# A gated FFT convolution, forward and backward: ScalarE's 4 KB transfers on SyncE's queue, gradients stored by channel halves, taps loaded into 32 rows, a new order

## The chip, the cores and the metric

The kernel runs on one core of one Trainium2 chip. A core has a matrix engine (TensorE, PE in the profile; its weight loads are PEld), VectorE (DVE), ScalarE (ACT), GpSimd (POOL) and SyncE (SP), and 16 DMA engines that move data between memory and the core's buffer. Each engine works off its own list of instructions in program order. SyncE and ScalarE issue transfers, each on a queue of its own (q1 and q10 in the page). The metric is the device time of one execution in microseconds.

## The reference

The sequence has 2048 positions and D = 512 channels; the feed-forward part has F = 1376 columns. `q`, `k`, `v` and `grad_out` are bfloat16 arrays of 2048 x 512.

```python
def _A_ref(q, k, v, shift_k, ssm_k, ssm_D):
    for t in range(4):                      # four taps per channel, along the sequence
        k_shift = k_shift + k_pad[:, t:t + S, :] * shift_k[:, 3 - t]
    kv = k_shift * v
    kv_f = rfft(kv padded to 4096); kf_f = rfft(ssm_k padded to 4096)
    y = irfft(kv_f * kf_f)[:2048]           # a long convolution, per channel
    return q * (y + kv * ssm_D)

def _B_ref(x, w_gate, w_up, w_down):
    return (sigmoid(x @ w_gate) * (x @ w_up)) @ w_down

xn = _layernorm(q)
out = q + _A_ref(xn, k, v, shift_k, ssm_k, ssm_D) * silu(_B_ref(xn, w_gate, w_up, w_down))
```

The kernel returns `out` and the gradients of `q`, `k`, `v`, the taps `shift_k`, the long filter `ssm_k`, `ssm_D` and the three weight matrices: `out_0`, then `out_1` to `out_9` in this order.

## The kernel before

**Layout.** Position 16p + j lies in partition p, slot j (`cview`, NJ = 16). The channels are worked in four groups of 128 (`NG`, `GW`). A Fourier transform of length 4096 is done as matmuls with constant tables: `step1`, a transpose by VectorE in 32 x 32 blocks (`flip`) and `step2` one way, `inv2` and `inv1` back. The spectra of the long filter (KD) and of the value path (VD) are written to memory on the way forward and loaded again on the way back, in two halves for each group.

**Stages.** First come the input loads, the layer norm of the first rows, and constant tables made by GpSimd and VectorE out of index patterns (`gen_fft_tables`, `gen_fft_consts`), while TensorE multiplies zeros (`warm`) until the first real matmul. Then the gate and up projections and the forward convolution, interleaved; then the backward pass of the feed-forward part. The last stage, from about 290 us on, has three parts that run interleaved:

- `dW` computes the weight gradients. Its operand tiles come by transposing loads from memory (`hD`, `dgD`, `duD`; the last twelve are `duD`) into three buffers. Its results go through five output buffers (`ot_r`), and ScalarE issues their stores (`out_7` to `out_9`, 128 KB each).
- `frontC` takes the gradient of the convolution's output through the forward transform, group by group.
- `backC` does the rest of the backward convolution, group by group: it loads the filter rows `ksh` (512 KB, one piece of 4 KB for each partition), multiplies the spectra, transforms back, writes the value gradient in place in `y2A`, stores the filter gradient `out_5` (512 KB, again 4 KB pieces), and computes the key gradient `dk` in `zA`. `ksh` and `out_5` are issued by ScalarE. The value gradient `out_3` is stored at the last group, whole; the key gradient `out_2` at the last group in two halves of the slots.

**The taps.** Four loads put the 4 x 512 taps of each group into one row each (rows 0, 32, 64, 96) of a tile `skr` that GpSimd has cleared (a memset of 128 x 2048). A matmul with 32 rows of ones (`ones1`) spreads them over all partitions (`skbc`).

**What sets the order.** A recorder (`Rec`) collects the operations of all stages with their numbers. Then `order` lays them out by tables of numbers: `ORDER` has one list for each engine, in which `a+n` stands for a, a+1, ..., a+n, and a list "moves" that fixes the order of the transfers over all queues. An evacuation of an accumulator (`evac`) goes to ScalarE or VectorE, by the list in which its number stands. A second table, `BANKS`, gives each accumulator its place. All instructions are issued in `emit`, so that every row of the profile has its line, L506.

Of the kernel before, what the change touches and what calls it, by code (L numbers as in the profile page):

```python
# [26 lines left out]
NG = 4  # L27
GW = D // NG
# [47 lines left out]
    """,  # L76
    "vector": """
# [555 lines left out]
def kernel_impl(ctx, tc, A_q, A_k, A_v, A_shift_k, A_ssm_k, A_ssm_D, B_x, B_w_gate, B_w_up, B_w_down,  # L633
                grad_out, out_0, out_1, out_2, out_3, out_4, out_5, out_6, out_7, out_8, out_9):
    nc = tc.nc
# [730 lines left out]
    def backC():  # L1366
        for cg in range(NG):
# [32 lines left out]
            if cg == NG - 1:  # L1400
                nc.sync.dma_start(o3C, y2A)
# [127 lines left out]
```

## Time and profile before

| what | value |
|---|---|
| median of three runs | 455.55 us (455.09, 455.55, 455.56) |
| the profiled execution | 456.14 us |
| its span, from the first to the last instruction | 454.3 us |
| mean granted TensorE clock | 0.996 of full speed |
| TensorE busy | 439.6 us (97% of the span) |
| VectorE busy | 410.4 us (90%) |
| ScalarE busy | 287.7 us (63%) |
| GpSimd busy | 23.2 us (5%) |
| data moved by DMA | 117.13 MB, mean 258 GB/s |
| share of the 16 DMA engines' span, SyncE's queue and ScalarE's | 89.3% and 6.6% |

Times are microseconds from the start of the span. A row of the timeline gives the start, the length, the engine, the operation with its tiles (result <- source), and in brackets the idle time of the engine before it and what ended that. `slab` is the one buffer in which all tiles lie; names such as `KD`, `duD` and `kshD` are arrays in memory, and `out_dram` any output. A wait is put down to what came last. A row with `x2` and more joins neighbours of one form. The share of the DMA engines can stand a little above 1 in a window.

### The profile page before, as it was taken

The numbers are of one execution on the slowest core, as the hardware profiler recorded it, in microseconds if no ns is written. First come the engines' busy times: TensorE is split into PE (matmuls) and PEld (weight loads), VectorE is DVE, ScalarE is ACT, GpSimd is POOL, SyncE is SP. The second block draws the span as 40 slices with busy tenths as digits, with TensorE's granted clock in tenths as the row PEclk, the third lists the DMA queues.
The fourth block names the chain that finished last, engine by engine and source line by source line (L and its number), as shares of the span: only waits on it lengthen the run. The fifth ranks groups of instructions, "written<-read, shape, count | busy, mean of one in ns | idle before, by whom it ended". The sixth has DMA issues, their size and how long they took to land.

```text
span 454.3 us, 11795 instructions
## 1 busy us (share of the span) xinstructions
PE 439.6 (97%) x4996; PEld 305.8 (67%) x5031; DVE 410.4 (90%) x620; ACT 287.7 (63%) x357; POOL 23.2 (5%) x49
## 2 busy tenths in 40 slices
PE   7999999999999999999999999999999999699997
PEld 3786686777768668566665755445577888588796
DVE  7899998999989999999999897779899999599992
ACT  4788788979787446973654433447567756475432
POOL 6501020000000000000000000000000000000000
PEclk9899999999999999999999999999999999999999
DMA  7988999649659889999998999899999999999996
GB/s 268 301 281 224 283 342 301 200 164 279 215 193 302 242 227 210 300 299 326 295 313 240 304 257 255 251 269 226 264 233 211 287 226 221 266 183 286 194 335 239
DMA packets 188678, 117.13 MB, mean 258 GB/s; under 512 B 107418, under 2 KB 174930, under 8 KB 188114
## 3 DMA queue, kind: packets, MB, share of 16 engines
q1 hardware_dynamic: 178320, 107.56, 89.3%
q10 hardware_dynamic: 10306, 8.82, 6.6%
q8 instruction: 39, 0.64, 0.6%
q14 instruction: 13, 0.11, 0.1%
HBM read 43.74 MB, written 46.70 MB: 199 GB/s over the span
## 4 chain that ended last, share of the span: by engine, by line
PE 88%; DMA 4%; DVE 2%; ACT 2%; issue 1%; POOL 1%; SPq 0%; ACTq 0%; POOLq 0%; DVEq 0%
PE psum L506 88%; DVE slab L506 2%; DMA slab<-duD 2%; DMA slab<-KD 2%; ACT slab L506 2%; POOL slab L506 1%; SPq L506 0%; ACTq L506 0%; POOLq L506 0%; DVEq L506 0%; POOLq L1513 0%
## 5 line engine op out<-in xcount | busy, mean ns | idle before, releaser
L506 PE MATMUL psum<-slab 128*128 128x256 bf16 (+5 forms) x4996 | 439.6, 302 | 11.3 <-DVE slab L506 6.0
L506 PEld LDWEIGHTS <-slab 128*128 128x128 bf16 (+2 forms) x5031 | 305.8, 96 | 145.0 <-issue 38.4
L506 ACT CAST slab<-psum 128x1024 bf16<-128x1024 f32 (+3 forms) x227 | 197.3, 907 | 130.3 <-PE psum L506 103.9
L506 DVE TENSOR_TENSOR slab<-slab 128x1024 bf16<-128x1024 bf16 (+4 forms) x302 | 240.5, 832 | 14.3 <-ACT slab L506 6.2
L506 ACT ACTIVATE slab<-slab 128x512 bf16<-128x512 bf16 (+5 forms) x63 | 53.3, 875 | 23.1 <-DVE slab L506 22.5
L506 DVE STREAM_TRANSPOSE slab<-slab 128x1024 f32<-128x1024 f32 x48 | 64.7, 1354 | 2.6 <-PE psum L506 1.7
L506 DVE CAST slab<-psum 128x1024 bf16<-128x1024 f32 (+2 forms) x38 | 42.4, 1119 | 11.5 <-PE psum L506 11.2
L506 DVE TENSOR_TENSOR slab<-psum,slab 128x512 bf16<-128x512 f32 (+2 forms) x52 | 31.7, 612 | 6.7 <-ACT slab L506 5.4
L506 ACT ACTIVATE slab<-psum 128x512 bf16<-128x512 f32 (+1 forms) x48 | 27.4, 576 | 6.6 <-PE psum L506 6.4
L506 POOL MEMSET slab<- 128x128 bf16 (+4 forms) x11 | 6.0, 559 | 255.5 <-DVE slab L506 152.1
L506 POOL TENSOR_TENSOR slab<-slab 128x2 f32<-128x2 f32 (+3 forms) x11 | 11.0, 1006 | 100.2 <-DVE slab L506 100.1
L506 DVE SCALAR_TENSOR_TENSOR slab<-slab 128x2 f32<-128x2 f32 (+2 forms) x41 | 14.5, 363 | 0.3
L506 ACT ACT_TABLE_LOAD x10 | 12.8, 1283 | 1.9 <-PEq L1513 1.7
L506 DVE SCALAR_TENSOR_TENSOR slab<-psum,slab 128x512 bf16<-128x512 f32 x16 | 10.8, 686 | 1.2 <-ACT slab L506 1.1
L506 DVE TENSOR_SCALAR slab<-slab 128x512 bf16<-128x512 bf16 (+6 forms) x26 | 8.4, 335 | 2.9 <-POOL slab L506 2.8
L506 DVE BATCH_NORM_STATS2 slab<-slab 128x6 f32<-128x512 bf16 x16 | 10.7, 676 | 0.0
L506 ACT COPY slab<-psum 128x1024 bf16<-128x1024 bf16 (+2 forms) x9 | 7.5, 837 | 1.5 <-PE psum L506 1.5
L506 DVE COPY slab<-psum 128x512 bf16<-128x512 bf16 (+1 forms) x10 | 4.8, 494 | 0.1
L506 POOL TENSOR_SCALAR slab<-slab 128x1 f32<-128x1 f32 (+3 forms) x10 | 3.3, 337 | 0.4
L506 DVE BATCH_NORM_AGGREGATE slab<-slab 128x2 f32<-128x6 f32 x16 | 2.7, 172 | 0.1
L506 DVE MEMSET slab<- 32x192 uint32 (+3 forms) x10 | 1.6, 160 | 1.2 <-PEq L1513 0.9
L506 POOL IOTA slab<- 128x32 f32 (+3 forms) x8 | 2.1, 272 | 0.5 <-POOLq L1513 0.4
(12 smaller groups left out, 7.1 us busy)
## 6 DMA issues: line engine op xcount, KB each, us to landing
slab<-KD SPq DMA_DIRECT2D x16, 512.0 KB, 4.6
hD<-slab SPq DMA_DIRECT2D x8, 704.0 KB, 6.2
dgD<-slab SPq DMA_DIRECT2D x8, 704.0 KB, 5.3
duD<-slab SPq DMA_DIRECT2D x8, 704.0 KB, 5.2
slab<-in_A_k_dram SPq DMA_DIRECT2D x4, 1024.0 KB, 7.0
KD<-slab SPq DMA_DIRECT2D x8, 512.0 KB, 4.7
VD<-slab SPq DMA_DIRECT2D x8, 512.0 KB, 4.4
out_dram<-slab SPq DMA_DIRECT2D x16, 256.0 KB, 3.9
```

What stands on the lines that cost most here:

```text
L506: getattr(getattr(self.nc, eng), meth)(*[place(v) for v in a], **{x: place(v) for x, v in k.items()})
```

## The change

Six places in the code are edited, and the tables are replaced.

1. GpSimd's memset of `skr` is gone. Each tap load fills 32 rows with the same 4 x 128 taps (a source stride of 0), and `ones1` holds 1/32 in place of 1.
2. The loads of `ksh` go from ScalarE's queue to SyncE's.
3. So do the stores of `out_5`.
4. `out_3` leaves in two stores of 256 channels each, recorded at the second and at the fourth group, where it was one store.
5. `out_2` leaves in one store of 256 channels, recorded at the second group, and at the fourth in two stores of eight slots and 256 channels each; before, in two stores of eight slots and 512 channels.
6. All lists in `ORDER`, and `BANKS`, are new. The lists name 588 operations for VectorE before and 589 now, 394 and 385 for ScalarE, 5031 and 5031 for TensorE, 237 and 247 for SyncE, 45 and 44 for GpSimd. Some 50 evacuations change their engine.

```diff
 ORDER = {
     "tensor": """
-        28 19 26 25 22 17 20 24 7+7 21 160+7 170+7 16 15 23 44+3 27 49+3 198+7 187+7 257+7 122+15 236+15 179+7 207+7
+        18 25 16 24 7+7 159+7 26 169+7 28 27 49+3 44+3 15 17 19 22 235+15 23 293+7 21 256+7 321+7 301+7 312+7 265+7
...
@@ -863,15 +864,15 @@
     f_ld(1)
     ld_w(256, 768, nc.sync, nc.sync)
-    nc.gpsimd.memset(skr, 0.0)
     for r in range(4):
-        nc.sync.dma_start(skr[32 * r:32 * r + 1, r, :], A_shift_k[r * GW:(r + 1) * GW, :].rearrange("(o d) t -> o (d t)", o=1))
+        taps = A_shift_k[r * GW:(r + 1) * GW, :]
+        nc.sync.dma_start(skr[32 * r:32 * r + 32, r, :], bass.AP(taps.tensor, taps.offset, [[0, 32], [1, 4 * GW]]))
     ld_w(768, F, nc.sync, nc.sync)
...
-    nc.gpsimd.memset(ones1, 1.0)
+    nc.gpsimd.memset(ones1, 1.0 / 32)
@@ -1370,7 +1371,7 @@
             ksh = ksh_r.next()
-            nc.scalar.dma_start(ksh.rearrange("p j d -> p (j d)"), kshD[cg])
+            nc.sync.dma_start(ksh.rearrange("p j d -> p (j d)"), kshD[cg])
@@ -1397,8 +1398,8 @@
             nc.vector.tensor_tensor(dkv, dkv, ksh, ALU.mult)
-            if cg == NG - 1:
-                nc.sync.dma_start(o3C, y2A)
+            if cg % 2 == 1:
+                nc.sync.dma_start(o3C[:, :, c1 - 2 * GW:c1], y2A[:, :, c1 - 2 * GW:c1])
@@ -1409,7 +1410,7 @@
-            nc.scalar.dma_start(out_5[c0:c1, :], dKT.rearrange("p n j -> p (n j)"))
+            nc.sync.dma_start(out_5[c0:c1, :], dKT.rearrange("p n j -> p (n j)"))
@@ -1436,8 +1437,8 @@
-                if cg == NG - 1:
-                    nc.sync.dma_start(o2C[:, js, :], zA[:, js, :])
+                if cg % 2 == 1:
+                    nc.sync.dma_start(o2C[:, js, c1 - 2 * GW:c1], zA[:, js, c1 - 2 * GW:c1])
```

The tables' effect is seen in the order of the instructions. First SyncE's queue in the last stage, from the load of the value rows (`in_A_v`) of groups 2 and 3 on; `duD` are the transposing loads for `dW`, KD3 and VD3 the spectra of group 3, `in_A_k` the key rows, `slab<-slab` a shift of three rows between partitions. Before:

```order
L506 DMA slab_102<-in_A_v_dram 128x16x256
L506 DMA_TRANSPOSE slab_102<-duD0_97 128x8x256
L506 DMA slab_102<-slab_102 15x384
L506 DMA_TRANSPOSE slab_102<-duD1_98 128x8x256
L506 DMA slab_102<-KD3_64 128x2048 x2
L506 DMA slab_102<-in_A_k_dram 112x3x256
L506 DMA_TRANSPOSE slab_102<-duD0_97 128x8x256 x2
L506 DMA_TRANSPOSE slab_102<-duD1_98 128x8x256 x2
L506 DMA slab_102<-VD3_68 128x2048
L506 DMA slab_102<-in_A_k_dram 15x3x256
```

The same stretch now, up to the second half of the key spectrum (`kshD2` is the `ksh` load of group 2):

```order
L507 DMA slab_102<-in_A_v_dram 128x16x256
L507 DMA slab_102<-KD3_64 128x2048
L507 DMA_TRANSPOSE slab_102<-duD0_97 128x8x256
...
L507 DMA slab_102<-kshD2_59 128x2048
...
L507 DMA_TRANSPOSE slab_102<-duD1_98 128x8x256
L507 DMA out_5_dram<-slab_102 128x2048
L507 DMA_TRANSPOSE slab_102<-duD0_97 128x8x256
L507 DMA_TRANSPOSE slab_102<-duD1_98 128x8x256
L507 DMA_TRANSPOSE slab_102<-duD0_97 128x8x256
L507 DMA_TRANSPOSE slab_102<-duD1_98 128x8x256
L507 DMA_TRANSPOSE slab_102<-duD0_97 128x8x256
...
L507 DMA slab_102<-KD3_64 128x2048
```

The first load of KD3 has moved ahead of two transposing loads, the second one behind seven; `ksh` and an `out_5` store stand among them (a row shift and two key halos between these rows are left out).

Second, the end of the same queue, before:

```order
L506 DMA_TRANSPOSE slab_102<-duD0_97 128x8x128
L506 DMA slab_102<-slab_102 112x384
L506 DMA out_3_dram<-slab_102 128x8192
L506 DMA slab_102<-slab_102 15x384
L506 DMA_TRANSPOSE slab_102<-duD1_98 128x8x128
L506 DMA out_2_dram<-slab_102 128x4096 x2
```

and now:

```order
L507 DMA_TRANSPOSE slab_102<-duD1_98 128x8x256 x2
L507 DMA out_3_dram<-slab_102 2048x1x256
L507 DMA out_5_dram<-slab_102 128x2048
L507 DMA slab_102<-slab_102 112x384
L507 DMA_TRANSPOSE slab_102<-duD0_97 128x8x128
L507 DMA out_3_dram<-slab_102 2048x1x256
L507 DMA slab_102<-slab_102 15x384
L507 DMA_TRANSPOSE slab_102<-duD1_98 128x8x128
L507 DMA out_2_dram<-slab_102 2048x1x256
L507 DMA out_2_dram<-slab_102 128x8x256
L507 DMA out_5_dram<-slab_102 128x2048
L507 DMA out_2_dram<-slab_102 128x8x256
```

One half of `out_3` has moved ahead of the last pair of transposing loads, and two `out_5` stores have come onto this queue.

Third, VectorE at the start of the program (the TENSOR_SCALAR of 128x1024 are integer masks for the tables, BN_STATS and BN_AGGR the statistics of the layer norm), before:

```order
L506 TENSOR_TENSOR slab<-slab 128x1024
L506 MEMSET slab 128x1
L506 TENSOR_SCALAR slab<-slab 128x1024
L506 TENSOR_SCALAR slab<-slab 128x1
L506 MEMSET slab 128x1
L506 TENSOR_SCALAR slab<-slab 128x1024
L506 TENSOR_SCALAR slab<-slab 128x1
L506 BN_STATS slab<-slab 128x6
```

and now:

```order
L507 TENSOR_TENSOR slab<-slab 128x1024
L507 TENSOR_SCALAR slab<-slab 128x1024
L507 TENSOR_SCALAR slab<-slab 128x1
L507 MEMSET slab 128x1
L507 TENSOR_SCALAR slab<-slab 128x1
L507 BN_STATS slab<-slab 128x6
L507 BN_AGGR slab<-slab 128x2
L507 TENSOR_SCALAR slab<-slab 128x1
```

One of the two masks has moved from ahead of the first statistics to behind the second ones; on GpSimd the memset of 128x2048 is gone.

More of the change, by code (lines that the diff above doesn't have):

```diff
@@ L33 @@
     "tensor": """
[42 rows of a table removed]
[43 rows of a table added]
     """,
     "vector": """
[25 rows of a table removed]
[25 rows of a table added]
     """,
     "scalar": """
[17 rows of a table removed]
[17 rows of a table added]
     """,
     "gpsimd": """
-        57 90 56 63 29 88 30 73 34 38 99 89 100+1 91 102 104+1 92 106 108 110 107 112+1 111 109 87 145 82 118+1 230
-        120 93 103 504 915 1329 938 1660 1932 2264 3544 4846
+        56+1 29+1 91 87 63 38 34 98 118 99+1 86 89+1 101 88 117 103 92 104 102 105+1 108 144 111 81 107 110 109 112
+        229 503 119 937 914 1328 1659 1931 2263 3543 4847
     """,
     "sync": """
[10 rows of a table removed]
[11 rows of a table added]
     """,
     "moves": """
[13 rows of a table removed]
[12 rows of a table added]
     """,
@@ L155 @@
 BANKS = (
-    "32100212103013100001321000111011000111130200001000011101011001001001130011110001100001013101011002011011001011"
-    "00001111100021010101010100100101010011100110101101001000100101023110101012320101311010210121011131102101030101"
-    "12010100220010201210121010120030232010023212212321102320221212122102230001002033110221002132110212210122232100"
-    "00222301223012103100101012133301231"
+    "22302000232103101001321110100010000101130100101000011101011001001001223011100001100001013101011002011011001011"
+    "00001111101021010101010100100101010011000110101001101001100111032101101012333101211012301030100301000110123001"
+    "01010100021210201201321020211031232112222110202320212301223012122102032012002203110231002131210210202122030210"
+    "01203311103012103100101102210301313"
 )
```

213 rows, old and new, of the table ORDER are left out of this document.

## The prediction

> **What bounds the kernel now.** I read the page first, then its stages in a table of windows, then the chain of waits, then the timelines of the stretches where TensorE idles. Of the page:
>
> ```profile
> PE 439.6 (97%) x4996; PEld 305.8 (67%) x5031; DVE 410.4 (90%) x620; ACT 287.7 (63%) x357; POOL 23.2 (5%) x49
> PE   7999999999999999999999999999999999699997
> DVE  7899998999989999999999897779899999599992
> ```
>
> TensorE is busy for 439.6 of the span's 454.3 us, so 14.7 us is all that any change of waits can win. The slices say where: the first, the last, and one at about 386 us, in which VectorE falls too. By windows (columns: window, length, busy time of PE, PEld, DVE, ACT, POOL, granted clock, DMA share, GB/s):
>
> ```profile
> 7.00:13.80 6.80, 4.22 (x40) 2.45 (x39) 6.72 (x25) 5.27 (x6) 3.71 (x13) 1.00 1.00 307
> 13.80:17.20 3.40, 3.33 (x20) 2.58 (x20) 2.13 (x6) 1.38 (x3) 2.77 (x11) 0.50 1.06 368
> 340.00:380.00 40.00, 39.94 (x714) 32.32 (x715) 38.88 (x37) 27.42 (x33) 0.10 (x1) 1.00 1.13 241
> 386.00:398.00 12.00, 8.23 (x177) 6.36 (x176) 7.06 (x8) 4.65 (x7) 0.00 (x0) 1.00 1.11 261
> 398.00:424.00 26.00, 25.93 (x388) 21.03 (x386) 25.80 (x23) 15.68 (x17) 0.00 (x0) 1.00 1.13 232
> 427.00:451.00 24.00, 23.90 (x380) 21.23 (x379) 17.13 (x31) 7.61 (x13) 0.00 (x0) 1.00 0.98 293
> ```
>
> From 386 to 398 us TensorE is idle for 12.00 - 8.23 = 3.77 us; around it it is full. The chain of waits names a key-spectrum load, and after it a load for the weight gradients:
>
> ```profile
> 385.68 9.04 DMA slab<-KD
> 394.81 3.58 DVE slab L506 x4
> 413.42 10.18 DMA slab<-duD
> 425.70 25.21 PE psum L506 x397
> ```
>
> The timeline there (start, length, engine, and in brackets the idle time before it and what ended it):
>
> ```profile
> 375.30 0.62 SPq L506 DMA_DIRECT2D slab<-in_A_v_dram  x1
> 383.12 2.51 SPq L506 DMA_TRANSPOSE slab<-duD  x1
> 384.41 0.35 ACTq L506 DMA_DIRECT2D slab<-kshD  x1
> 384.86 0.39 ACTq L506 DMA_DIRECT2D out_dram<-slab  x1
> 385.68 1.83 SPq L506 DMA_DIRECT2D slab<-KD  x2
> 393.50 0.32 ACT L506 CAST slab<-psum 128x192 bf16<-128x192 f32 x1 [1.58 <-DMA out_dram<-slab]
> 394.81 1.23 DVE L506 TENSOR_TENSOR slab<-slab 128x2048 bf16<-128x2048 bf16 x1 [4.46 <-DMA slab<-KD]
> 393.58 1.75 PE L506 MATMUL psum<-slab 128*128 128x256 bf16 x41 [1.79 <-issue]
> 397.31 27.64 PE L506 MATMUL psum<-slab 32*32 32x512 bf16 x408 [1.97 <-DVE slab L506]
> 425.70 25.20 PE L506 MATMUL psum<-slab 128*128 128x128 bf16 x397 [0.76 <-ACT slab L506]
> ```
>
> Two causes stand side by side. VectorE waited 4.46 us for the first half of channel group 3's key spectrum, and TensorE then 1.97 us for VectorE. ScalarE's cast at 393.50 waited for a store of weight gradients to leave its buffer, and TensorE, whose accumulator that cast empties, 1.79 us (the profile says "issue"; the cast began 0.08 us before TensorE did). Together 3.76 us. What the transfers took from issue to landing:
>
> ```profile
> slab<-kshD ACTq DMA_DIRECT2D x1, 512.0 KB, 6.7
> slab<-KD SPq DMA_DIRECT2D x2, 512.0 KB, 9.0
> out_dram<-slab ACTq DMA_DIRECT2D x30, 128.0 KB, 4.9
> slab<-VD SPq DMA_DIRECT2D x1, 512.0 KB, 4.2
> ```
>
> The first two are of 380 to 400 us, the third is the kernel's median for such stores, the fourth a load of the same size at 408 us, when little else ran.
>
> **The change part by part.**
>
> *4 KB transfers off ScalarE's queue, and the store behind them.* The store at 384.86 stands right behind the 512 KB load of 384.41, which landed at 391.1; the cast got its buffer at about 393.5, 8.6 us after the store's issue. With the median of 4.9 us it would be free at 389.8, before the cast is due (393.50 - 1.58 = 391.92). So the 1.79 us go. The eight issues that leave ScalarE (0.35 us each) are worth nothing: it is busy for 63%. On SyncE they can hold up what stands behind them, which is the third item.
>
> *The key spectrum's first half, moved.* The first pair of listings under the change shows SyncE's queue here. The first KD3 load now precedes both transposing loads; its second half is gone from here. It was issued at 385.68, 0.05 us after the transpose before it was issued (383.12 + 2.51), so it waited for its place in the queue. Now it stands right behind the issue of the value load, which ended at 375.30 + 0.62, so it can go out at about 376; even with its old 9.0 us it lands at 385, against a need at 394.81 - 4.46 = 390.35: 5 us of cover. VectorE's wait goes, and with it TensorE's 1.97 us. Sum so far: -3.76. The bound on the other side is nothing gained, if the transposes behind it, which feed TensorE's filler work, become the late ones.
>
> *The second half.* It now follows the four transposes of the listing, a fifth and a halo. The four took, and the product that reads this half began:
>
> ```profile
> 393.30 14.41 SPq L506 DMA_TRANSPOSE slab<-duD  x4
> 408.39 0.43 SPq L506 DMA_DIRECT2D slab<-in_A_k_dram  x1
> 412.99 2.44 DVE L506 TENSOR_TENSOR slab<-slab 128x2048 bf16<-128x2048 bf16 x2
> ```
>
> On the old clock the four end at 407.71, a fifth at their mean of 3.60 at 411.31, the halo at 411.74; landing is 4.2 to 9.0 later, 415.9 to 420.7, so 2.95 to 7.75 us after 412.99. All of it shifts with TensorE, whose reads free the buffers. After the second KD load (385.68 + 1.83 = 387.51) no transpose went out until 393.30: TensorE had not freed a buffer. The queue was thus not full with work, and of the two landings the 4.2, from the same stretch of the kernel, is the nearer: VectorE waits 2.95 us. Of its 4.46 us TensorE lost 1.97, 44%; of 2.95 that is 1.3. I put +1.3, with 0 (an earlier fifth transpose) and 7.75 (nothing left to fill) as ends.
>
> *Stores by channel halves.* The two value and key gradients leave as 1 MB with 512-byte pieces. I have loads of these shapes:
>
> ```profile
> slab<-in_A_v_dram SPq DMA_DIRECT2D x2, 1024.0 KB, 6.4
> slab<-in_A_v_dram SPq DMA_DIRECT2D x1, 2048.0 KB, 10.1
> ```
>
> Two halves take 2 x 6.4 - 10.1 = 2.7 us more than the whole, for two arrays 5.4 us of queue time. The second pair of listings shows where they stand: one ahead of the last pair of transposes, one between the two, two behind, where one whole stood between and two halves behind. That pair feeds only the end of the last weight gradient. At the end TensorE computes without a break from 425.70 to 450.90, past the big stores, so less storing there brings nothing either. I take 0, up to +1.5 if the last pair is late by a quarter of 6.4. The 0.76 us before 425.70 I leave as they are; they may go.
>
> *Taps in 32 rows, no clearing of their tile.* The removed memset, and VectorE's integer mask beside it (two of one form, by groups of 4.6 to 5.2 us and of 5.43 to 7.5 us):
>
> ```profile
> 5.30 1.80 POOL L506 MEMSET slab<- 128x2048 bf16 x1
> L506 DVE TENSOR_SCALAR slab<-slab 128x1024 int32<-128x1024 int32 x1 | 0.7, 696 | 1.8 <-POOL slab L506 1.8
> L506 DVE TENSOR_SCALAR slab<-slab 128x1024 int32<-128x1024 int32 x1 | 2.3, 2300 | 0.0
> 11.38 0.61 PE L506 MATMUL psum<-slab 128*128 128x128 bf16 x5 [1.41 <-DVE slab L506]
> 12.82 0.84 PE L506 MATMUL psum<-slab 128*128 128x128 bf16 x12 [0.83 <-DVE slab L506]
> 13.87 4.30 PE L506 MATMUL psum<-slab 128*128 128x256 bf16 x27 [0.20 <-DVE slab L506]
> ```
>
> The same instruction takes 2.30 us beside the memset and 0.70 without: 1.60 us on VectorE, which then starts the layer norm for which TensorE waits 1.41 and 0.83 us. In the new order (third pair of listings) one mask stands behind the norm's statistics, so VectorE is early by more. I take -1.6; the ends are 0 (the projections' weights set the start) and -3.9, both waits and the half-rate clock of 13.80 to 17.20 gone (3.40 x 0.5 = 1.70). The four tap loads grow to 32 rows, which is 128 KB in all, no more than one of the stores above.
>
> *New order elsewhere.* From 340 to 380 us TensorE loses 0.06 us and the matmuls are the same ones, so there is nothing to win; 0, give or take 1.
>
> **Sum.** -3.76 + 1.3 + 0 - 1.6 = -4.06. The profiled execution took 456.14 us with 454.3 of span and so comes to 452.1; it lay 0.59 above the median of 455.55, which makes 451.5.
>
> **The rivals.**
>
> *Better still (447.1).* No wait for the second half, the 0.76 and all 3.9 at the start gone: -3.76 - 0.76 - 3.9 = -8.4. For it: each is a wait with a named end. Against: all must go at once.
>
> *The clock stays low longer (453.2).* In the new tensor table 12 warming matmuls come before the first transposes, not 17; the 17 and the load these wait for:
>
> ```profile
> 1.25 6.67 PE L506 MATMUL psum<-slab 128*128 128x512 bf16 x17 [1.25 <-DVE slab L506]
> 8.12 1.85 PE L506 MATMUL psum<-slab 128*128 128x128 bf16 x19 [0.20 <-DMA slab<-in_A_ssm_k_dram]
> ```
>
> Twelve, at 6.67 / 17 = 0.39 each, end at 1.25 + 4.7 = 6.0; the load came at 8.12: 2.1 us of idling. The clock fell to 0.50 once after 6.80 us in which TensorE was busy for 4.22, so another such stretch costs 1.70. The Trainium skill ("TensorE: Matmul & The Clock Gate", Part 1) says the clock halves after one idle window of about 3.4 us, free-running; the stretch of 3.40 us at 0.50 agrees in length, and by that rule 2.1 us of idling need not trip it.
>
> *The queue is the limit (455.2).* DMA share is 1.11 to 1.13 in these stages, and on SyncE's queue two moved transfers of 512 KB now stand ahead of the four transposes; before, one of them moved its data on ScalarE's queue beside SyncE's. If they hold the transposes back in full, 4.2 us each, VectorE waits 2.95 + 8.4 = 11.35 us for the second half, and 44% of it is 5.0: -3.76 + 5.0 - 1.6 = -0.4. The wait has moved and the change does not do what it says. For it: the landings of 6.7 and 9.0 us side by side. Against: at 340 to 380 us the same share leaves TensorE whole, and the transposes waited for buffers until 393.30 anyway. The Trainium skill ("DMA: Bandwidth & Descriptors", Queues, rings and completion order) speaks for this rival: each DMA engine takes turns between the queues' packets, but works off one queue in its order. By that rule a transfer on a queue of its own slows the other, and on the same queue it stops it; no row of this kernel shows the second.
>
> *The second half decides (457.9, slower).* A landing of 9.0 us makes VectorE wait 7.75 at about 409; if the filler is used up, TensorE loses all of it: 7.75 - 5.36 = +2.4. It decides from a loss of 5.4 us on. For it: 10.18 us for a `duD` load in the chain. Against: TensorE lost 44% of such a wait before.
>
> **How the numbers follow.** Forecast 44%, better still 12%, clock 9%, queue 18%, second half 17%. The forecast's own range is 449.5 to 453.5; with the rivals 447.0 to 457.0. A difference under 0.2% (0.9 us) can't be told from none. Faster by more: 44 + 12 + 9 and 3 of the queue's 18, 68%; its other 15 within; slower 17%.
>
> **What would show it.** The windows 380 to 400 with no idle PE; no wait of VectorE for KD above 3 us, and its place after 400 if there is one; ScalarE's cast not waiting for `out_dram`; the first 128x256 matmuls about 1.6 us earlier than 13.87, with both masks of 0.7 us. A wait for `duD` in the chain of over 3 us, or a first 24 us in which PE does less, makes it wrong.

## The result, and the profile after

The changed kernel takes 449.0 us (median of four runs, 448.0 to 450.02); the kernel before, run on the same chip, 455.32 (454.43 to 455.56). The ratio is 0.9865, with a 95% interval of 0.9837 to 0.9893: 6.1 us less, between 4.9 and 7.4. The forecast was 451.5 and -4.06. The profiled execution took 450.02 us (456.14 before) with a span of 447.7 (454.3). The ratios leave out executions that are over 1.5% above the fastest of their kernel; the profile of the last experiment, with four places changed, is of such a one, so its idle time is not compared below.

The page of the changed kernel, busy times and slices:

```profile
PE 435.3 (97%) x4994; PEld 304.1 (68%) x5031; DVE 407.1 (91%) x621; ACT 286.6 (64%) x356; POOL 22.7 (5%) x48
PE   8999999999999999999999999999999999899995
DVE  8999999999988699999999887789799899899993
```

The one low slice of TensorE, at about 386 us, reads 8 where it read 6, and the first reads 8 and not 7. The same windows as before, with the last one cut at 447 us, where the span ends:

```profile
7.00:13.80 6.80, 6.55 (x78) 5.04 (x80) 6.44 (x15) 6.24 (x8) 4.89 (x19) 1.00 1.04 365
13.80:17.20 3.40, 3.40 (x45) 3.14 (x43) 2.71 (x10) 3.03 (x6) 1.92 (x6) 1.00 0.88 244
340.00:380.00 40.00, 40.00 (x667) 32.66 (x665) 37.94 (x36) 26.99 (x32) 0.73 (x1) 1.00 1.12 247
386.00:398.00 12.00, 12.00 (x202) 10.32 (x202) 11.97 (x14) 6.41 (x10) 0.00 (x0) 1.00 1.12 236
398.00:424.00 26.00, 26.00 (x434) 20.81 (x432) 24.73 (x22) 17.78 (x21) 0.00 (x0) 1.00 1.15 248
427.00:447.00 20.00, 16.13 (x255) 14.27 (x253) 12.96 (x27) 5.45 (x9) 0.00 (x0) 0.98 1.01 269
```

Two things are new. From 7.00 to 13.80 us TensorE is busy for 6.55 us and not for 4.22, and the stretch at half clock from 13.80 to 17.20 is gone (1.00 for 0.50). From 386 to 424 us it has no idle time left. The timelines of TensorE, ScalarE and SyncE at the places that the prediction spoke of (a `q` behind the engine marks the issue of a transfer):

```profile
1.26 5.09 PE L507 MATMUL psum<-slab 128*128 128x512 bf16 x12 [1.26 <-DVE slab L507]
7.09 3.54 PE L507 MATMUL psum<-slab 128*128 128x128 bf16 x47 [0.74 <-DMA slab<-in_A_ssm_k_dram]
10.79 24.54 PE L507 MATMUL psum<-slab 128*128 128x256 bf16 x288 [0.16 <-issue]
375.44 4.78 SPq L507 DMA_TRANSPOSE slab<-duD  x1
384.49 0.38 ACTq L507 DMA_DIRECT2D out_dram<-slab  x1
384.91 1.50 ACT L507 CAST slab<-psum 128x1024 bf16<-128x1024 f32 x2 [3.65 <-DMA out_dram<-slab]
385.97 57.16 PE L507 MATMUL psum<-slab 128*128 128x96 bf16 x912 [1.82 <-ACT slab L507]
388.44 13.95 SPq L507 DMA_TRANSPOSE slab<-duD  x5
403.12 0.34 SPq L507 DMA_DIRECT2D slab<-KD  x1
```

The first 128x256 matmuls start at 10.79 us and not at 13.87. One stall of TensorE is left in the last stage, 1.82 us. TensorE ends at 385.97 + 57.16 = 443.13 us; before, at 425.70 + 25.20 = 450.90. From there to the end of the span it is 4.6 us, and was 3.4. The chain of waits says what is behind the stall and what ends last:

```profile
375.44 9.02 DMA slab<-duD
384.91 1.02 ACT slab L507
385.97 36.80 PE psum L507 x619
...
435.01 7.32 DMA out_dram<-slab
```

**Where the time went** is best read at equal work. The trace has all 5031 weight loads of TensorE; each belongs to a matmul of known columns. At the moments at which both kernels have done the same share of these columns (the zeros left out), the changed kernel is ahead by:

```
time before, us    23.7   116.9   218.0   318.7   370.8   449.1
lead, us            4.5     5.0     5.0     4.5     4.8     7.7
```

So 4.5 us come from the first 24 us, next to nothing from the middle, about 2.9 from the last stage, behind 371 us, and 1.2 go again behind TensorE's end: 7.8 at its end (450.90 - 443.13), 6.6 in the span. TensorE's idle time from 374 us on says the same of the last stage: 4.60 us before (1.79 + 1.97 + 0.76, and a gap of 0.07) and 1.82 now.

**One thing in the listing that the prediction had left out.** The listing of a kernel's instructions can also name what each waits for. One row of SyncE's list and two neighbours on ScalarE's, of the changed kernel:

```
L507 DMA_TRANSPOSE slab_102<-duD0_97 128x8x256 [waits DMAHW1_49,PE_49]
...
L507 DMA out_7_dram<-slab_102 128x2x256 [waits DMAHW1_49]
L507 CAST slab_102<-psum_106 128x1024 [waits PE_49]
```

Every transfer of SyncE and ScalarE signals its end on one of eight counters (DMAHW0 to 7), handed out when the program is built; the trace has their landings on eight semaphores, too. A transfer that gets a counter in use waits on its engine's list until the transfer that uses it has landed, and all that stands behind it on that list waits too. The first row is the transposing load of 375.44; it lands at 375.44 + 9.02 = 384.46. The second is the store of 384.49, whose data had been ready since 371.13. Behind it stands the cast for which TensorE waited; by itself it waits for TensorE's data alone. This is the 1.82. The same is in the profile before:

```profile
423.63 0.43 ACTq L506 DMA_DIRECT2D out_dram<-slab  x1
```

This store on ScalarE's list went out right after the `duD` load of the chain, which has its counter, had landed at 413.42 + 10.18 = 423.60, and the cast behind it cost the 0.76 us.

### The profile page after: what moved, and what is told of

It is laid out like the page before. It is cut to its first block, busy times and chain, and to the rows that moved or that the text cites. A ratio compares the mean times of both kernels' runs of the same rounds, so it can differ in the third digit from the quotient of the medians.

```text
span 447.7 us, 11823 instructions
## 1 busy us (share of the span) xinstructions
PE 435.3 (97%) x4994; PEld 304.1 (68%) x5031; DVE 407.1 (91%) x621; ACT 286.6 (64%) x356; POOL 22.7 (5%) x48
## 4 chain that ended last, share of the span: by engine, by line
PE 87%; DMA 5%; DVE 3%; ACT 2%; issue 1%; ACTq 1%; POOL 0%; SPq 0%; DVEq 0%
PE psum L507 87%; DVE slab L507 3%; DMA slab<-duD 2%; ACT slab L507 2%; DMA out_dram<-slab 2%; DMA slab<-in_A_ssm_k_dram 1%; ACTq L507 1%; POOL slab L507 0%; SPq L507 0%; DVEq L507 0%
## 5 line engine op out<-in xcount | busy, mean ns | idle before, releaser
L507 PEld LDWEIGHTS <-slab 128*128 128x128 bf16 (+3 forms) x5031 | 304.1, 96 | 138.9 <-issue 36.4
L507 ACT CAST slab<-psum 128x1024 bf16<-128x1024 f32 (+4 forms) x230 | 199.2, 908 | 130.3 <-PE psum L507 103.2
L507 ACT ACTIVATE slab<-slab 128x512 bf16<-128x512 bf16 (+5 forms) x61 | 51.5, 878 | 17.2 <-DVE slab L507 17.0
L507 DVE CAST slab<-psum 128x1024 bf16<-128x1024 f32 (+3 forms) x35 | 39.0, 1128 | 9.5 <-PE psum L507 7.2
L507 POOL MEMSET slab<- 128x128 bf16 (+3 forms) x10 | 4.4, 437 | 276.6 <-DVE slab L507 139.5
L507 POOL TENSOR_TENSOR slab<-slab 128x2 f32<-128x2 f32 (+3 forms) x11 | 11.9, 1089 | 78.7 <-DVE slab L507 78.7
L507 DVE TENSOR_SCALAR slab<-slab 128x512 bf16<-128x512 bf16 (+6 forms) x28 | 7.4, 282 | 0.2
L507 ACT COPY slab<-psum 128x1024 bf16<-128x1024 bf16 (+2 forms) x7 | 5.3, 771 | 2.7 <-PE psum L507 2.7
L507 DVE COPY slab<-psum 128x512 bf16<-128x512 bf16 (+1 forms) x12 | 6.1, 527 | 0.9 <-PE psum L507 0.9
```

Of the source, the lines that this page charges most:

```text
L507: getattr(getattr(self.nc, eng), meth)(*[place(v) for v in a], **{x: place(v) for x, v in k.items()})
```

## The experiments

All twelve were timed in five rounds beside the kernel before, in three groups, each on one chip. On these chips the kernel before spread more, so that a ratio is known to 0.3 to 0.5%, 1.4 to 2.4 us. "Lead" is read as above, against the same trace of before; "idle" is TensorE's idle time (all gaps over 0.05 us) from 374 us to its end, in the one profiled execution.

### The taps' part alone

```diff
-    nc.gpsimd.memset(skr, 0.0)
-        nc.sync.dma_start(skr[32 * r:32 * r + 1, r, :], ...)
+        nc.sync.dma_start(skr[32 * r:32 * r + 32, r, :], bass.AP(taps.tensor, taps.offset, [[0, 32], [1, 4 * GW]]))
-    nc.gpsimd.memset(ones1, 1.0)
+    nc.gpsimd.memset(ones1, 1.0 / 32)
```

The tables are those of before, with all numbers behind the memset's lower by one.

> The kernel before with the taps' part of the change alone: no memset of the tap tile, each tap load fills 32 rows, the ones become 1/32; every table as before, with the memset's number taken out. As predicted (VectorE's mask slowed by GpSimd's memset, 2.30 us against 0.70): the first projections start 1.6 us earlier and the time falls by 1.6, to about 453.8. If the stretch at half clock goes as well: by 3.3, to about 452.1. If the early gain of the changed kernel (4.6 us by the time TensorE has done the work that it had done at 24 us) comes from the new order: 0 to 0.5 us.

Measured: ratio 1.0023 (0.999 to 1.0057): no gain. In the profile the lead is -1.5 us at 24 us, a loss, and still -1.4 at 449. The groups of VectorE from 4 to 8 us, and TensorE's timeline:

```profile
L503 DVE TENSOR_SCALAR slab<-slab 128x1024 int32<-128x1024 int32 x2 | 1.4, 691 | 1.8 <-POOL slab L503 1.8
```

```profile
7.98 2.40 PE L503 MATMUL psum<-slab 128*128 128x128 bf16 x24 [0.85 <-DMA slab<-in_A_ssm_k_dram]
11.21 0.40 PE L503 MATMUL psum<-slab 128*128 128x128 bf16 x4 [0.83 <-DVE slab L503]
14.84 1.38 PE L503 MATMUL psum<-slab 128*128 128x128 bf16 x13 [3.23 <-ACT slab L503]
```

Both masks now take 0.69 us and TensorE's wait of 1.41 is gone (the one of 0.83 is not): the predicted mechanism works. But a new wait of 3.23 us for ScalarE has come. ScalarE's queue shows it:

```profile
5.46 2.19 ACT L503 ACTIVATE slab<-slab 128x1024 bf16<-128x1024 int32 x2 [2.45 <-DVE slab L503]
11.25 0.39 ACTq L503 DMA_DIRECT2D slab<-in_B_w_up_dram  x1
11.69 1.15 ACT L503 ACTIVATE slab<-slab 128x1024 f32<-128x1024 int32 x1 [4.05 <-DVE slab L503]
```

Without the memset the tap loads no longer wait, the transfers go out in another order, and the counters fall differently: the load of the up weights on ScalarE's list now has that of a load which landed at 11.23, where before it had one that was free at 8.71 (it went out at 8.73 then). It stands ahead of ScalarE's activations.

### The same, with that load moved

```diff
 "scalar":
-    1 68 65+1 3 61 177 62
+    1 68 3 65+1 61 177 62
 "moves":
-    1 0 68 70 4 43 148 233 72 2 3 76
+    1 0 68 70 4 3 43 148 233 72 2 76
```

> The kernel before with the taps' part of the change, and with one load moved: the first columns of the up weights, which ScalarE issues, become the sixth transfer and not the eleventh, ahead of ScalarE's first activation. In the run with the taps alone this load waited on ScalarE's list until 11.25 us for the counter of a load that landed at 11.23, the activations behind it started late, and TensorE waited 3.23 us for ScalarE. If that wait ate the gain: it goes, the first projections start 1.6 to 3.3 us earlier than before, and the time is 1.6 to 3.3 us below the kernel before. If the weights' landing sets the start: within 0.9 us of the kernel before.

Measured: 0.9991 (0.9961 to 1.002). The start went as expected:

```profile
11.22 0.84 PE L503 MATMUL psum<-slab 128*128 128x128 bf16 x12 [0.83 <-DVE slab L503]
12.27 3.57 PE L503 MATMUL psum<-slab 128*128 128x256 bf16 x40 [0.20 <-DVE slab L503]
```

The projections begin at 12.27, which is 1.60 us earlier than before, and the half clock is gone as well (1.00 from 13.80 to 17.20). The lead, 3.2 us at 18 us, is 1.6 at 24 and still at 371 us: what the clock gave was lost again by 24 us. Short waits of TensorE between 15.8 and 20.8 us make 0.5 us of that; where the rest went its idle time doesn't show. Then the last stage took most of the lead: 0.3 at 407 us, 1.2 at 449. Its profile there:

```profile
384.91 8.25 DMA slab<-KD
...
393.25 2.45 DVE slab L503 x3
...
395.75 53.93 PE psum L503 x805
```

TensorE waited 3.51 us behind the same key-spectrum load that cost 1.97 before, and ran at half clock for 3.41 us after it (397.08 to 400.49). In the time itself the 1.6 us don't show.

### The new order for the first 40 us, and for the first 150

The code of the run with the taps alone. Each engine's list begins with what the changed kernel starts on it before the stated time, in the changed order; behind it the rest follows in the order of before. The accumulators of these operations have the changed places.

> The kernel before with the taps' part, and with the new order and the new accumulator places for all that the changed kernel starts in its first 40 us; behind that the old order. If the gain of the start keeps its size to the end: 4.6 us less than before, about 450.8, with no half clock after 13 us. If the later stages wait for something that the start doesn't set, less. Against the run with the taps alone it shows what the order does there: by the prediction (1.6 us in all from this part) next to nothing, by the traces 1.3 to 3 us.

> As the run with the new order for the first 40 us, but with it for all that the changed kernel starts in its first 150 us, so that the seam between the orders lies in a stage where TensorE has its next work ready (the seam at 41 to 55 us cost 2.1 us of the 4.9 gained). If the start is the larger part of the change's gain: TensorE is 4.9 us ahead at 150 us and still at 370 us, the last stage loses what it lost before (3 to 4.5 us of waits), and the time is 4 to 5 us below the kernel before. The rival, that a lead of the start is given back in the last stage, where the transfers set the pace (as in the run with one load moved: 1.63 ahead at 370 us, 0.32 at 406): 2 us or less.

Measured: 0.9943 (0.991 to 0.9975) with the first 40 us, 0.9924 (0.9895 to 0.9954) with the first 150: 2.6 us less (1.1 to 4.1) and 3.5 (2.1 to 4.8). The leads:

```
time before, us    23.7   116.9   218.0   318.7   370.8   406.8   449.1
first 40 us         4.9     2.9     2.9     2.9     2.9     1.6     2.6
first 150 us        4.7     5.3     4.6     4.4     4.4     5.2     6.1
```

The lead of the start is there, 4.7 to 4.9, and lasts to the end, less what the seam costs; it isn't given back. So the start is the larger part of the change's gain. The taps alone gained nothing, and with the order they did; the order without the taps' part was not run, so how the two share the gain is not shown. In the last stage, in the old order, VectorE waited 4.1 and 2.9 us for `KD` in these two runs.

### The key spectrum's first half moved, and nothing else

```diff
 "sync":
-    4845 5327 4609 5328 4950 5160
+    4845 4950 5327 4609 5328 5160
```

(and the same move in "moves"; 4950 is the load, 5327 and 5328 are the transposing loads).

> The kernel before with one transfer moved: the first half of the key spectrum of group 3 goes out right behind the value rows, ahead of two transposing loads and a row shift. As predicted: VectorE's wait of 4.46 us and TensorE's 1.97 us go, and so the time falls by about 2.0, to 453.4; the cast that waits for a store (1.79) stays. The rival, that the eight completion counters or the queue are the limit: the transposing loads come later by what the load takes, TensorE waits for them in its place, and the time moves by less than 0.9 either way.

Measured: 1.0007 (0.9976 to 1.0038). In the profile VectorE's wait for `KD` is gone, as predicted, and the lead is 2.0 us at 407. But then:

```profile
392.64 1.75 PE L503 MATMUL psum<-slab 128*128 128x256 bf16 x41 [0.36 <-issue]
395.29 27.64 PE L503 MATMUL psum<-slab 32*32 32x512 bf16 x408 [0.90 <-DVE slab L503]
424.38 22.80 PE L503 MATMUL psum<-slab 128*128 128x128 bf16 x343 [1.45 <-ACT slab L503]
```

1.79 + 1.97 + 0.76 = 4.52 us of stalls have become 0.36 + 0.90 + 1.45 = 2.71. The lead at the end is 1.3, and in the time nothing shows. The transfer is the right one to move, but alone it isn't worth 2.0 us that can be measured.

### The 4 KB transfers on SyncE's queue alone, and back on ScalarE's

```diff
-            nc.scalar.dma_start(ksh.rearrange("p j d -> p (j d)"), kshD[cg])
+            nc.sync.dma_start(ksh.rearrange("p j d -> p (j d)"), kshD[cg])
-            nc.scalar.dma_start(out_5[c0:c1, :], dKT.rearrange("p n j -> p (n j)"))
+            nc.sync.dma_start(out_5[c0:c1, :], dKT.rearrange("p n j -> p (n j)"))
```

First in the kernel before; then, undone (with - and + exchanged), in the changed kernel, beside which the changed kernel itself was run once more.

> The kernel before with the key rows' loads (ksh) and the filter gradient's stores (out_5) issued by SyncE, all eight at the place that they had in the order of the transfers. As predicted: the 128 KB store behind the ksh load lands in 4.9 us and not 8.6, the cast's wait of 1.58 and TensorE's 1.79 us go, about 453.6. The rival (what holds the store is not the queue but what else is under way, and a store on ScalarE's list waits for a completion counter as before): less than 0.9 us, with a wait of a cast for a store in the same stretch.

> The changed kernel with the eight 4 KB transfers issued by ScalarE again, each at the place on its list at which SyncE issued it; the order of the transfers as in the changed kernel. As predicted (a 512 KB load ahead of a store on ScalarE's queue delays the store and the cast that needs its buffer): 1.8 us slower than the changed kernel. The rival, that the queue is no matter and the counters are: within 0.9 us, unless one of the eight has to wait for its counter on ScalarE's list, which the trace would show as a gap of ScalarE ahead of it.

> The changed kernel once more, unaltered, so that the runs beside it have a neighbour on the same chip: 6.3 us below the kernel before, give or take 1.4.

Measured: before with the transfers on SyncE's queue 0.9987 (0.9957 to 1.0017); the changed kernel with them back on ScalarE's 0.9877 (0.9837 to 0.9917), against 0.9861 (0.9825 to 0.9896) unaltered. The queue makes no difference that can be told; the first interval reaches from 2.0 us less to 0.8 more, so that the 1.8 us of the prediction are not ruled out by the times alone. From the profile of the first of these runs: two casts of ScalarE, one by its row and one by the waits from 378 to 440 us, and TensorE's row behind the second:

```profile
392.89 0.54 ACT L504 CAST slab<-psum 128x192 bf16<-128x192 f32 x2 [1.48 <-PE psum L504]
ACT slab L504 <- DMA out_dram<-slab: 3.7, 1, 3.7
413.99 33.25 PE L504 MATMUL psum<-slab 128*128 128x256 bf16 x496 [1.93 <-ACT slab L504]
```

At the predicted place the wait is gone. By the trace's semaphores the store of 384.94 landed at 389.42, 4.48 us after its issue, where the one before took 8.62 (384.86 to 393.48); the cast at 392.89 waits for TensorE alone, and the stall of 1.79 us is not there. (The transposing load issued beside it landed sooner as well, after 5.7 us and not 10.1, so the queue's share in this can't be told apart.) But 20 us later, at 413.36, another cast had waited 3.7 us, behind a store that went out at 412.88, 0.02 us after the `VD` load that uses its counter had landed, and TensorE 1.93 us for that cast. In the second, ScalarE's store at 387.00 went out as the same transposing load had landed (386.93), and TensorE stood 2.64 us at 390 and 2.15 us at 428 for `duD` loads.

The unaltered kernel's second profile is the surprise: not one gap of TensorE over 0.05 us from 374 us to its end at 441.66. Here the transposing load landed at 380.62, six and not nine us after its issue, and the store went out at 380.96. The lead of this execution is 5.0 us at 24 us, 4.5 at 371 and 9.2 at 449, so 4.7 us of it come from the last stage. The 1.82 us belong to one execution, not to the kernel.

### Cast and store exchanged

```diff
 "scalar":
-    5327 5217 5107 5447+1
+    5327 5107 5217 5447+1
```

> The changed kernel with two neighbours on ScalarE's list exchanged: a cast of the forward transform, for which TensorE waited 1.82 us at 384 us, now stands ahead of the store of a weight gradient that went out at 384.49, 0.02 us after a transposing load had landed whose completion counter it uses. If the wait for that counter is the cause: the cast starts at about 381.3 and not at 384.91, TensorE's 1.82 us go, and the time is 1.8 us below the changed kernel's. If the cast waits for something else (the data of another engine, its own buffer), or the next store takes the wait over: less than 0.9 us.

Measured: 0.9866 (0.9837 to 0.9895), no difference from the changed kernel. ScalarE's timeline, and TensorE's:

```profile
381.26 1.01 ACT L505 CAST slab<-psum 128x1024 bf16<-128x1024 f32 x1 [1.22 <-PE psum L505]
384.40 0.38 ACTq L505 DMA_DIRECT2D out_dram<-slab  x1
384.88 0.59 ACT L505 CAST slab<-psum 128x512 bf16<-128x512 f32 x1 [2.60 <-DMA slab<-slab]
```

```profile
375.80 12.71 PE L505 MATMUL psum<-slab 128*128 128x256 bf16 x260
391.35 52.91 PE L505 MATMUL psum<-slab 128*128 128x256 bf16 x822 [2.83 <-DMA slab<-duD]
```

The cast starts at 381.26, as expected, while the store still waits until 384.40: that the counter held both is shown. But TensorE, let through there, ran up against the next transposing load, which went out at 383.28 and landed at 391.30, and waited 2.83 us. The wait moved, it didn't go.

### Stores whole again, a store earlier, and four places at once

```diff
-            if cg % 2 == 1:
-                nc.sync.dma_start(o3C[:, :, c1 - 2 * GW:c1], y2A[:, :, c1 - 2 * GW:c1])
+            if cg == NG - 1:
+                nc.sync.dma_start(o3C, y2A)
-                if cg % 2 == 1:
-                    nc.sync.dma_start(o2C[:, js, c1 - 2 * GW:c1], zA[:, js, c1 - 2 * GW:c1])
+                if cg == NG - 1:
+                    nc.sync.dma_start(o2C[:, js, :], zA[:, js, :])
```

> The changed kernel with the value and key gradients stored as before: out_3 whole and out_2 in two halves of the slots, each at the place of the last store of its array; the two early stores are taken out of the lists. As predicted: no difference beyond 0.9 us, since TensorE computes past these stores. The rival from the traces: from TensorE's end to the end of the span the changed kernel takes 4.6 and 4.8 us where it was 3.4, because eight stores stand on the queues in the last 10 us; if the stores by halves are to blame, this run's end is back at 3.4 and the time 1.2 us lower; if the early halves help, its end is longer.

```diff
 "sync":
-    5745 5884 4610 5379 5903 6076 5906 5904 6077 4845 6115
+    5745 5884 4610 4845 5379 5903 6076 5906 5904 6077 6115
```

> The changed kernel with one store moved: the first half of out_2, whose data are ready at 406 us and which goes out at 433, goes out right behind the first half of out_3 (at about 421), ahead of the last two pairs of transposing loads. If the transfers under way set the end: from TensorE's end to the end of the span 3.4 in place of 4.6 us, about 1 us less in all. The rival, that the 1 MB delays the transposing loads for which TensorE waits: a wait for duD between 425 and 437 us, and 1 us more.

```diff
 "scalar":
-    3918+1 3865 4002 4080
+    3918+1 4002 4080 3865
-    5327 5217 5107 5447+1
+    5327 5107 5217 5447+1
 "sync":
-    5328 4608 4851 4849 5329
+    5328+1 4608 4851 4849
-    4610 5379 5903 6076 5906 5904 6077 4845
+    4610 4845 5379 5903 6076 5906 5904 6077
```

> The changed kernel with four places changed: the exchange of cast and store at 384 us; a store at 308 us behind two casts instead of ahead of them (TensorE waited 0.58 to 0.95 us there); the transposing load of 382 us directly behind the one of 375 us, ahead of a row shift, the key rows and a halo (TensorE waited 2.83 us for it in the run with the exchange); and the early store of out_2 at 421 us. If these waits are what is left to win: TensorE idle under 1 us between 374 and 440 us, and 1 to 3 us below the changed kernel. If the last stage is bound by what the queue moves, whichever transfer comes first: another wait of the same size, and within 0.9 us.

Measured: 0.9888 (0.9835 to 0.994) with whole stores, 0.9871 (0.9828 to 0.9915) with the earlier store, 0.9899 (0.987 to 0.9929) with all four places. None can be told from the changed kernel, and none beats it. With whole stores it is 5.2 us from TensorE's end (441.77) to the end of the span (447.0): in this profile the longer end is there without the halves. With the earlier store it is 3.0, but there TensorE itself ends late, at 446.85:

```profile
386.09 52.76 PE L505 MATMUL psum<-slab 128*128 128x96 bf16 x823 [2.96 <-ACT slab L505]
440.57 6.29 PE L505 MATMUL psum<-slab 128*128 128x96 bf16 x89 [1.72 <-DMA slab<-duD]
```

The 1.72 us for `duD` are the rival of that expectation, a little behind the 425 to 437 us that it named.

### The last stage over all profiles

TensorE's idle time from 374 us on, us:

```
old order there:  before 4.6   taps 3.7   taps, load moved 3.6   first 40 us 3.1   first 150 us 1.8
                  KD alone 2.9   4 KB alone 4.2
new order there:  changed 1.8   again 0.0   whole stores 0.8   exchange 2.8   earlier store 4.7
                  4 KB back 5.3
```

The changed order, left alone, has 0 and 1.8; small edits to it bring 0.8 to 5.3. Seven profiles of the old order have 1.8 to 4.6.

## Why the prediction was right, and where it was not

The sign was right, and 449.0 us lies in the range with the rivals (447.0 to 457.0), but half a us under the forecast's own (449.5 to 453.5). The sum was some 2 us short, and its terms were not those that came. For the last stage it had -3.76 + 1.3 = -2.46; TensorE's idle time there fell by 2.8 us in one profile of the changed kernel and by 4.6 in the other. That this is near is in part luck: the +1.3 did not come, and the -1.79 is not shown to come from its cause.

- **Taps and the start (-1.6).** The term that was mis-sized: it measured -4.5, beyond its own end of -3.9. Its mechanism was right where nothing else holds the start (masks of 0.69 us, projections 1.60 us earlier in the run with the load moved). What was missed is the order. In the changed kernel the projections start 3.08 us earlier and the half clock doesn't come (1.70). The chain before ran through GpSimd's and VectorE's tables up to 13.87 us; the chain after is the `ssm_k` load and then TensorE without a break (the three rows at 1.26, 7.09 and 10.79). The bound of -3.9 took the waits and the clock, but held the first transposes at 8.12; they came at 7.09, since the load landed a microsecond earlier among other neighbours. The listing of VectorE shown ahead of the prediction had it: statistics of the layer norm stand before the second mask. The prediction read it as "early by more" and took 1.6.
- **The key spectrum's first half (-1.97).** Right in the mechanism: in the five profiles of the changed order that have the transfers on SyncE's queue VectorE waits 0.9 us at most for `KD`, and 2.0 to 4.5 in all profiles that have it in the old place. Alone it is worth about 1.3 us at TensorE's end (one profile), and the time does not show it.
- **4 KB transfers off ScalarE's queue (-1.79).** Not shown as a gain, and incomplete as a mechanism. The step that failed is "So the 1.79 us go", worked out from the store's landing alone. The store did land soon with the queue freed (4.48 us), and its stall went. But a store on ScalarE's list also waits for its completion counter: in the run with the queue alone such a wait cost TensorE 1.93 us 20 us later, and in the changed kernel's first profile 1.82 us in the old place; in its second profile neither stall came. Both runs that moved only the queue showed no difference in time, to within some 2 us.
- **The second half (+1.3).** Did not come. It went out at 403.12 and not at 411.7: the five transposing loads began 4.9 us earlier and took 13.95 us, 2.8 each for 3.60. That "TensorE had not freed a buffer" until 393.30 was wrong for the end of that wait: TensorE's last signal ahead of it came at 391.58, and what ended it, at 393.23, was the landing of the transposing load that had the counter.
- **Stores by halves (0).** Right for TensorE; the end behind it grew by 1.2 us, which the prediction had not counted and which the run with whole stores doesn't explain by the halves. ScalarE's last store went out 0.62 us behind TensorE's end (0.30 before) and took 3.0 us to land (1.67 before). Just ahead of it ScalarE's list had stood for a counter once more: its store of 442.41 went out when the store of 435.01, the chain's last row, had landed at 442.33. Why that last store took longer is open.
- **The 0.76 us** were left as they are and went.
- **The rivals.** Low clock at the start: no run with the new order there has a granted clock under 1.00 in its first 24 us. The second half late: no. The queue as the limit: its time did not come, nor VectorE's wait for the second half. But its "the wait has moved" holds for single moves in the last stage: the exchange and the earlier store each brought a wait for a `duD` load, and with the key spectrum moved alone 2.71 of 4.52 us of stalls stayed, one of them grown from 0.76 to 1.45. The larger gain came from the start, which doesn't depend on it.
- **The signs.** `KD`'s wait and the masks came as said, and the first 128x256 matmuls came 3.08 us earlier, not 1.6. In the first profile two signs failed: TensorE idled in the window from 380 to 400 us, and ScalarE's cast waited for `out_dram`. A `duD` load (9.02 us) also stands in its chain, with 3.65 us of idle time of ScalarE behind it, which by the last sign speaks against the prediction. In the second profile none of the three is there.

**What stays open:** how much of the 2.9 us of the last stage (4.7 in the second profile) is the changed order's and how much the single execution's. The difference in time between the changed kernel (0.9861) and the run with only its first 150 us (0.9924) is 2.9 us, known to 1.6 and 1.4 us each, from two groups of runs.

## What to carry to other kernels

Before a wait is put down to slow data, list which completion counter each transfer uses: a store with old data that goes out in the very moment at which an unrelated load lands is waiting for that load's counter, and holds everything behind it on its engine's list. Price a new order by comparing, at the start, the chain of waits that it leaves, not only the instruction that was taken out: here the removed memset was worth nothing in the time until the lists behind it had changed. And where a stage's stalls differ by 1.8 us between two executions of one program, one profile can't give a term of 2 us; profile it again.

## What the runs showed of the hardware

**The length of a stall doesn't decide whether half clock follows it.** After stalls of TensorE of 1.80 us (first 150 us in the new order) and 2.64 us (4 KB back on ScalarE's queue) the windows read:

```profile
380.00:400.00 20.00, 18.20 (x298) 14.23 (x297) 17.00 (x17) 11.52 (x16) 0.00 (x0) 0.91 1.10 258
```

```profile
380.00:400.00 20.00, 17.02 (x282) 13.79 (x280) 15.16 (x15) 9.10 (x12) 0.00 (x0) 1.00 1.11 225
```

The shorter stall was followed by some 3.4 us at a granted clock of 0.50, which makes the mean of 20 us 0.91; the longer one was not. The Trainium skill ("TensorE: Matmul & The Clock Gate", Part 1) has a free-running window of about 3.4 us, and half clock after at least one idle window. The length agrees here; that it takes a whole idle window does not, since a stall of 1.80 us was enough. So a stall in this kernel costs its own length or that and up to 1.7 us more (3.4 x 0.5).

**The issue of a transposing load holds SyncE for long.** The one at 375.44 is recorded with 4.78 us for its issue, the five behind it with 2.8 each, the plain load at 403.12 with 0.34. What stands behind on SyncE's list goes out that much later: the next transfer behind the one of 375.44 went out at 380.28, right after 375.44 + 4.78 = 380.22.
